# Loads on GpSimd's queue, and later operands in the model that orders TensorE: a scan and two layers on one core

## The chip, the core and the metric

The kernel runs on one core of a Trainium2 chip. The core has five engines that run side by side: TensorE (PE, matrix products; PEld is its loading of weights), VectorE (DVE), ScalarE (ACT), GpSimd (POOL) and SyncE (SP), which issues DMAs. Each engine takes its instructions in the order in which they stand in its queue, and waits for semaphores at the head of it. The metric is the device time in microseconds of one execution; less is better.

## The reference

A chunked scan over 4 x 8 sequences of 768 steps (head size 32, state size 16, chunks of 32), then two layers with a hidden width of 2048 over the 3072 tokens of width 256:

```
per chunk:  L   = causal * exp(cum_i - cum_j)
            y   = ((C B^T) * L) x  +  (C state) * exp(cum)
            state = exp(sum la) * state + sum_j B_j x_j exp(cum_end - cum_j)
x1 = leaky(y  @ w_in)  @ w_out          # leaky(h) = max(0.01 h, h)
x2 = relu(x1 @ w2_in)^2 @ w2_out
```

All inputs and the output are float32.

## The kernel before

The tokens are cut into 12 pieces of 256, three to a sequence group; in each piece 16 chunks of 32 steps lie side by side in 128 partitions. `scan_piece(p)` loads two tensors (in1: B, C, x; in2: decays and B), scales them by powers of two so that each is the sum of two half-precision parts, and has three groups of small products on TensorE: the **attention product** (L632 and L633, from the diagonal tile kbd into S), the **inside product** (L675 to L677, from xbh and xbl into Y) and the **carried product** (L714 and L715, from sbd into Y). The diagonal tiles hold blocks of 32 x 32 on a diagonal, so that one product serves four chunks; from piece 1 on, SyncE fills each with a group of four DMAs (`diag`, L556), and piece 0 does it with copies on DVE and ACT. The result of a piece goes to yh and yl (ACT L721 the rounded part, DVE L726 the rest), which the layers read. `sequence_scales` loads a whole sequence group five times in parts (L453) for its largest values.

The layers run in phases over one piece (256 tokens) or two (512). A phase has rounds of first products into hp (L761 to L763), the activation on ACT and DVE (gh, t, gl), second products into o (L792 and L793) and last products (L799). Every float32 product is made of three products of rounded parts; the weights are loaded as words (`load_w`, L294), and split by ACT (L309, L315, L353) and DVE (L328, L332, L357) into a rounded part and the rest.

The order of all this is not written by hand. `Plan.op` records each operation with its engine, an estimate of its duration, what it reads and writes; `Plan.order` runs a model of the engines: an operation is ready at the end of what it reads plus HOP (0.12), each engine takes the ready operation that must be done earliest (`lateness`, less a lead of 30 or 10 us for the scan), and buffers come free when their last reader is done. The program is then issued in the order of that model, so each engine's queue holds its instructions in that order. In the model SyncE issues a load in 0.06 us, and a group of four diagonal copies is one operation of 2.6 us that keeps SyncE for 0.3. All DMAs stand in SyncE's queue.

## Time and profile before

| | us |
|---|---|
| median of 3 runs | 672.5 (670.22 to 672.55) |
| the profiled execution | 672.55, of which its span 670.8 |
| PE busy | 603.6 (90% of the span) |
| DVE, ACT busy | 418.2 (62%), 362.7 (54%) |
| POOL busy | 5.2 (1%) |
| mean granted clock of TensorE | 0.977 |

The span is from the first to the last instruction. A row of the timeline has its start, its duration, the engine, the line of the kernel, the operation, what it writes from what it reads, the shapes, how many were merged into the row, and in brackets how long the engine sat idle before it and what ended that. "DMA kbd<-kmx" as what ended a wait is the landing of a diagonal copy. A wait is put down to what came last.

### The profile page before, as it was taken

To read this page: it belongs to the slowest core of one execution; us is meant where nothing else is said; L and a number is where in the kernel's file an instruction comes from. 1 tells how busy PE (TensorE), PEld (TensorE's weight loads), DVE (VectorE), ACT (ScalarE), POOL (GpSimd) and SP (SyncE) were. 2 spreads that over 40 slices of the span, in tenths; PEclk is the share of its full clock that TensorE was granted. 3 is DMA by queue.
4 is the path that set the end of the run, shared out by engine and by line. 5 is a ranking of instruction groups with operands and counts; after the bars stand their busy time and mean duration, and the time that the engine had idled before them with its cause. 6 is when DMAs were issued, how large, how long until landed. Compare 5 with 4: busy or idle time off the path is not lost.

```text
span 670.8 us, 11009 instructions
## 1 busy us (share of the span) xinstructions
PE 603.6 (90%) x4248; PEld 514.4 (77%) x4248; DVE 418.2 (62%) x735; ACT 362.7 (54%) x639; POOL 5.2 (1%) x14
## 2 busy tenths in 40 slices
PE   1378779899999998989999979999989999999997
PEld 0277669798887898877888767888767888888885
DVE  8968968689888546688423758522765422444553
ACT  5967845658765444555444545444644444444442
POOL 3000000000000000000000000000000000000000
PEclk9997979899999999999999989999989999999999
DMA  8565662542133334443000143100210000000000
GB/s 325 185 155 168 188 176 48 148 80 86 49 52 102 100 85 84 128 91 43 30 31 1 41 89 38 40 32 1 49 16 9 0 32 0 1 0 1 33 0 32
DMA packets 111252, 46.46 MB, mean 69 GB/s; under 512 B 94304, under 2 KB 100064, under 8 KB 111200
## 3 DMA queue, kind: packets, MB, share of 16 engines
q1 hardware_dynamic: 111200, 45.76, 27.0%
q8 instruction: 33, 0.54, 0.3%
q14 instruction: 19, 0.16, 0.1%
HBM read 36.83 MB, written 3.15 MB: 60 GB/s over the span
## 4 chain that ended last, share of the span: by engine, by line
PE 66%; DMA 11%; DVE 10%; ACT 6%; SPq 4%; issue 3%; DVEq 0%; ACTq 0%
PE hp L761 11%; PE o L799 10%; PE hp L762 10%; PE hp L763 10%; PE o L792 10%; PE o L793 10%; SPq L556 4%; DMA sbd<-t 3%; DMA in<-in 3%; DMA kbd<-kmx 2%; DVE gl L780 1%; DMA wst<-w2o 1%; DMA wst<-w1o 1%; ACT wst L315 1%; ACT wst L309 1%
## 5 line engine op out<-in xcount | busy, mean ns | idle before, releaser
L780 DVE TENSOR_TENSOR gl<-t,gh 128x512 fp32r<-128x512 f32 x192 | 131.6, 687 | 128.0 <-ACT gh L774 84.5
L761 PE MATMUL hp<-yl,wh1i 128*128 128x256 f32 (+1 forms) x288 | 96.3, 334 | 3.9 <-DVE yl L726 2.1
L763 PE MATMUL hp<-yh,wl1i 128*128 128x256 f32 (+1 forms) x288 | 95.3, 331 | 0.2 <-DVE wl1i L357 0.2
L762 PE MATMUL hp<-yh,wh1i 128*128 128x256 f32 (+1 forms) x288 | 95.3, 331 | 0.0
L792 PE MATMUL o<-gh,wl1o 128*128 128x256 f32 (+1 forms) x288 | 89.6, 331 | 4.8 <-DVE wl1o L357 4.2
L779 ACT CAST gh<-t 128x512 fp32r<-128x512 f32 x96 | 58.9, 619 | 63.0 <-DVE t L778 46.5
L774 ACT ACTIVATE gh<-hp 128x512 fp32r<-128x512 f32 x96 | 57.4, 598 | 61.2 <-PE hp L763 31.5
L793 PE MATMUL o<-gh,wh1o 128*128 128x256 f32 (+1 forms) x288 | 88.3, 327 | 0.0
L775 ACT ACTIVATE t<-hp 128x512 f32<-128x512 f32 x96 | 57.0, 598 | 57.2 <-PE hp L763 56.2
L777 ACT ACTIVATE t<-hp 128x512 f32<-128x512 f32 x96 | 57.3, 598 | 51.7 <-PE hp L763 49.1
L778 DVE TENSOR_TENSOR t<-t 128x512 f32<-128x512 f32 x96 | 65.5, 688 | 30.9 <-ACT t L777 30.6
L792 PE MATMUL o<-gh,w2o 128*128 128x512 f32 x192 | 76.8, 400 | 0.0
L761 PE MATMUL hp<-yl,wh2i 128*128 128x512 f32 x192 | 76.6, 399 | 0.0
L793 PE MATMUL o<-gh,w2o 128*128 128x512 f32 x192 | 76.0, 396 | 0.0
L763 PE MATMUL hp<-yh,wl2i 128*128 128x512 f32 x192 | 75.7, 394 | 0.0
L762 PE MATMUL hp<-yh,wh2i 128*128 128x512 f32 x192 | 75.5, 393 | 0.0
L799 PE MATMUL o<-gl,wh1o 128*128 128x256 f32 (+1 forms) x288 | 63.8, 332 | 2.4 <-DVE gl L780 2.3
L761 PEld LDWEIGHTS hp<-yl,wh1i 128*128 128x128 f32 x288 | 57.6, 200 | 9.1 <-DVE yl L726 2.2
L792 PEld LDWEIGHTS o<-gh,wl1o 128*128 128x128 f32 x288 | 56.5, 196 | 10.0 <-DVE wl1o L357 4.8
L763 PEld LDWEIGHTS hp<-yh,wl1i 128*128 128x128 f32 x288 | 57.8, 201 | 4.7 <-DVE wl1i L357 0.4
L762 PEld LDWEIGHTS hp<-yh,wh1i 128*128 128x128 f32 x288 | 57.7, 200 | 4.3
L799 PE MATMUL o<-gl,w2o 128*128 128x512 f32 x192 | 60.8, 398 | 0.0
(124 smaller groups left out, 935.2 us busy)
## 6 DMA issues: line engine op xcount, KB each, us to landing
in<-in SPq DMA_DIRECT2D x12, 640.0 KB, 4.3
in<-in SPq DMA_DIRECT2D x12, 512.0 KB, 3.4
all<-in SPq DMA_DIRECT2D x15, 384.0 KB, 3.8
wst<-w1i SPq DMA_DIRECT2D x8, 512.0 KB, 5.5
wst<-w1o SPq DMA_DIRECT2D x8, 512.0 KB, 5.8
wst<-w2i SPq DMA_DIRECT2D x8, 512.0 KB, 4.0
out_t<-ob SPq DMA_DIRECT2D x12, 256.0 KB, 2.2
wst<-w2o SPq DMA_DIRECT2D x5, 512.0 KB, 3.6
```

Source lines behind the costliest of these rows:

```text
L761: nc.tensor.matmul(hp, wh, xl[:, :, k], start=(k == 0), stop=False)
L762: nc.tensor.matmul(hp, wh, xh[:, :, k], start=False, stop=False)
L763: nc.tensor.matmul(hp, wl, xh[:, :, k], start=False, stop=(k == KI - 1))
L774: op("ACT", 0.6, lambda: nc.scalar.activation(gh(), h(), AF.Lrelu), r=[h], w=[gh], busy=0.52)
L775: op("ACT", 0.6, lambda: nc.scalar.activation(t(), h(), AF.Lrelu), r=[h], w=[t], busy=0.52)
L777: op("ACT", 0.6, lambda: nc.scalar.activation(t(), h(), AF.Relu), r=[h], w=[t], busy=0.52)
L778: op("DVE", 0.69, lambda: nc.vector.tensor_tensor(t(), t(), t(), ALU.mult), w=[t])
L779: op("ACT", 0.62, lambda: nc.scalar.copy(gh(), t()), r=[t], w=[gh], busy=0.55)
L780: op("DVE", 0.69, lambda: nc.vector.tensor_tensor(gl(), t(), gh().bitcast(F32), ALU.subtract), r=[t, gh], w=[gl])
L792: nc.tensor.matmul(o[d]()[:, : self.n], wl, gh()[:, c], start=(m == 0), stop=False)
L793: nc.tensor.matmul(o[d]()[:, : self.n], wh, gh()[:, c], start=False, stop=False)
L799: nc.tensor.matmul(o[d]()[:, : self.n], wh, gl()[:, c], start=False, stop=(m == KO - 1))
```

## The change

Two things are changed. The loads of weights, of the sequence groups and of all pieces but the first are issued from GpSimd's queue in place of SyncE's; the model gets GpSimd as an engine that takes 1.0 us for each. And in the model, an operation of TensorE sees what another engine made not 0.12 us after its end but 2.0 us in the scan pieces from 1 on, and 0.4 us in the layers. SyncE keeps the loads of piece 0, the diagonal copies and the stores of the output. What each instruction computes is as before; added lines move the numbers of all lines behind them by 6 to 8.

```diff
+HOP_SCAN, HOP_LAYERS = 2.0, 0.4
 HOP = 0.12
...
-        o.lead = self.lead
+        o.lead, o.hop = self.lead, self.hop_pe
...
+    def hop(self, y, b):
+        if y.kb:
+            return HOP + 0.5
+        if y.engine == b.engine:
+            return -y.us if y.engine == "PE" else 0.0
+        return b.hop if b.engine == "PE" else HOP
+
...
-        free = {e: 0.0 for e in ("PE", "DVE", "ACT", "SP")}
+        free = {e: 0.0 for e in ("PE", "DVE", "ACT", "SP", "POOL")}
...
-                        at = max(
-                            ends[y] + HOP if y.engine != b.engine or y.kb else 0.0 if y.engine == "PE" else ends[y]
-                            for y in b.before
-                        )
+                        at = max(ends[y] + self.hop(y, b) for y in b.before)
...
-        op("SP", 0.06, lambda: nc.sync.dma_start(st(), w_dram[nm][sl]), w=[st], kb=512 if j is None else 256)
+        op("POOL", 1.0, lambda: nc.gpsimd.dma_start(st(), w_dram[nm][sl]), w=[st], kb=512 if j is None else 256)
...
-                nc.sync.dma_start(t(), all_[:, :, U * at : U * (at + 16)])
+                nc.gpsimd.dma_start(t(), all_[:, :, U * at : U * (at + 16)])
...
-            op("SP", 0.06, load, w=[t], kb=384)
+            op("POOL", 1.0, load, w=[t], kb=384)
...
-        op("SP", 0.06, lambda: nc.sync.dma_start(v(), in1[p]), w=[(v, k) for k in ("x", "b", "ct")], kb=640)
-        op("SP", 0.06, lambda: nc.sync.dma_start(w(), in2[p]), w=[(w, k) for k in ("az", "bt")], kb=512)
+        e, us, q = ("SP", 0.06, nc.sync) if p == 0 else ("POOL", 1.0, nc.gpsimd)
+        op(e, us, lambda: q.dma_start(v(), in1[p]), w=[(v, k) for k in ("x", "b", "ct")], kb=640)
+        op(e, us, lambda: q.dma_start(w(), in2[p]), w=[(w, k) for k in ("az", "bt")], kb=512)
...
     weights()
+    plan.hop_pe = HOP_SCAN
...
-    plan.lead = 0.0
+    plan.lead, plan.hop_pe = 0.0, HOP_LAYERS
```

What this does to the queues, at three places. DVE at the start, from the maxima of piece 0 (mx) on; lt and e are its two scans, behind the clip of the decays (d1e, in_122 or in_124), wst is the first weight. Before:

```order
L405 TENSOR_REDUCE mx<-in_120 128x1 x3
L590 TENSOR_SCALAR d1e<-in_122 128x16
L591 TENSOR_SCALAR in_122<-in_122 128x16x31
L592 MEMSET in_122 128x16
L250 TENSOR_REDUCE pm<-ident 128x1
L598 SCALAR_TENSOR_TENSOR lt<-in_122,delta 128x512
L491 TENSOR_REDUCE m_154<-S 3x1
L603 SCALAR_TENSOR_TENSOR e_156<-in_122,d1e 128x512
L492 TENSOR_SCALAR dg<-ident,m_154 3x3
L328 SCALAR_TENSOR_TENSOR wst<-wst 128x512
```

Now:

```order
L411 TENSOR_REDUCE mx<-in_120 128x1 x3
L256 TENSOR_REDUCE pm<-ident 128x1
L497 TENSOR_REDUCE m_148<-S 3x1
L498 TENSOR_SCALAR dg<-ident,m_148 3x3
L334 SCALAR_TENSOR_TENSOR wst<-wst 128x512
L505 TENSOR_SCALAR eb<-S 128x3
L597 TENSOR_SCALAR d1e<-in_124 128x16
L598 TENSOR_SCALAR in_124<-in_124 128x16x31
L599 MEMSET in_124 128x16
L508 TENSOR_SCALAR eb<-eb 128x3
L605 SCALAR_TENSOR_TENSOR lt<-in_124,delta 128x512
```

The first weight's merge moved ahead of the clip and of both scans. The second place is the queue of the loads while pieces 0 and 1 are scanned; wst are weights, and the numbers are those of the buffers. On SyncE before:

```order
L294 DMA wst_352<-w1i 128x2x256
L556 DMA kbd_95<-kmx_440 32x16x32 x4
L556 DMA xbh_93<-xh_442 32x16x32 x4
L556 DMA xbl_94<-xl_469 32x16x32 x4
L294 DMA wst_543<-w1o 128x512
L294 DMA wst_589<-w1i 128x2x256
```

On GpSimd now:

```order
L459 DMA all_154<-in1 128x3x256
L524 DMA in1_255<-in1 128x1280
L525 DMA in2_314<-in2 128x1024
L300 DMA wst_320<-w1i 128x2x256
L300 DMA wst_415<-w1o 128x512
L300 DMA wst_444<-w1i 128x2x256
L300 DMA wst_471<-w1o 128x512
```

The copies are gone from between the loads; they stand alone in SyncE's queue, and eight weights stand ahead of these rows in GpSimd's. The third place is TensorE where the attention product of piece 9 begins (L632, now L639). Before:

```order
L761 MATMUL hp_4818<-yl_2613,wh2i_114 128x512
L762 MATMUL hp_4818<-yh_2597,wh2i_114 128x512
L763 MATMUL hp_4818<-yh_2597,wl2i_115 128x512
L632 LDWEIGHTS kbd_95
L632 MATMUL S_4831<-ch_4752,kbd_95 128x32
L633 LDWEIGHTS kbd_95
L633 MATMUL S_4831<-cl_4768,kbd_95 128x32
```

Now:

```order
L799 MATMUL o0_4809<-gh_4799,w2o_1974 128x512
L800 MATMUL o0_4809<-gh_4799,w2o_1974 128x512
L799 MATMUL o1_4812<-gh_4799,w2o_1974 128x512
L800 MATMUL o1_4812<-gh_4799,w2o_1974 128x512
L806 MATMUL o0_4809<-gl_4825,w2o_1974 128x512
L806 MATMUL o1_4812<-gl_4825,w2o_1974 128x512
L639 LDWEIGHTS kbd_95
L639 MATMUL S_4855<-ch_4727,kbd_95 128x32
L640 LDWEIGHTS kbd_95
L640 MATMUL S_4855<-cl_4773,kbd_95 128x32
```

Before, the attention product stands right behind a first product of layer 2, and the second and last products of the first three rounds of that phase come after it; now these three rounds' second and last products stand ahead of it, and one first product less.

## Rows read from the trace of the kernel before

**Rows 1.** Windows: stretch, its length, busy us of each engine, PEclk, DMA share, GB/s.

```profile
32.70:150.00 117.30, 96.70 (x943) 92.18 (x944) 94.24 (x182) 75.44 (x138) 0.00 (x0) 0.91 0.54 135
150.00:510.00 360.00, 343.63 (x2511) 289.72 (x2510) 225.07 (x380) 192.00 (x343) 0.00 (x0) 0.99 0.25 57
510.00:671.00 161.00, 156.65 (x679) 127.30 (x677) 69.59 (x101) 69.52 (x116) 0.00 (x0) 1.00 0.03 10
```

**Rows 2.** Waits of PE: engine, tile, line, what ended them: us, times, longest.

```profile
PE S L632 <- DMA kbd<-kmx: 17.4, 6, 5.4
...
PE Y L714 <- DMA sbd<-t: 5.6, 9, 1.6
...
PE o L792 <- DVE wl1o L357: 4.2, 3, 2.8
PE Y L676 <- DVE mkl L665: 3.4, 5, 1.0
```

**Rows 3.** Timeline of PE: the rows ahead of which it waited longest.

```profile
48.90 0.58 PE L792 MATMUL o<-gh,wl1o 128*128 128x256 f32 x1 [2.81 <-DVE wl1o L357]
...
87.03 0.19 PE L632 MATMUL S<-ch,kbd 128*128 128x32 f16 x1 [5.43 <-DMA kbd<-kmx]
...
122.21 0.18 PE L632 MATMUL S<-ch,kbd 128*128 128x32 f16 x1 [3.24 <-DMA kbd<-kmx]
...
265.68 0.18 PE L632 MATMUL S<-ch,kbd 128*128 128x32 f16 x1 [2.65 <-DMA kbd<-kmx]
...
283.89 0.18 PE L714 MATMUL Y<-qh,sbd 128*128 128x32 f16 x1 [1.64 <-DMA sbd<-t]
...
291.95 0.18 PE L632 MATMUL S<-ch,kbd 128*128 128x32 f16 x1 [1.48 <-DMA kbd<-kmx]
...
392.10 0.18 PE L632 MATMUL S<-ch,kbd 128*128 128x32 f16 x1 [2.39 <-DMA kbd<-kmx]
...
492.56 0.18 PE L632 MATMUL S<-ch,kbd 128*128 128x32 f16 x1 [2.24 <-DMA kbd<-kmx]
```

**Rows 4.** Windows of the stretches behind two of these waits.

```profile
283.90:290.40 6.50, 6.50 (x56) 5.20 (x56) 6.50 (x12) 4.29 (x8) 0.00 (x0) 1.00 0.45 47
392.10:397.50 5.40, 5.40 (x45) 4.46 (x46) 2.75 (x7) 0.00 (x0) 0.00 (x0) 0.68 0.63 143
```

**Rows 5.** Timeline of SP (its first weight load) and of POOL (its last instruction).

```profile
1.65 0.69 SPq L294 DMA_DIRECT2D wst<-w1i  x1
...
5.79 0.15 POOL L254 MEMSET dec<- 128x32 f32 x1
```

**Rows 6.** Timeline of SP: the copy groups of piece 1, first row, and the next load.

```profile
34.16 2.73 SPq L556 DMA_DIRECT2D kbd<-kmx  x4
...
42.42 0.56 SPq L294 DMA_DIRECT2D wst<-w1o  x1
```

**Rows 7.** DMA issues: line, count, KB each, median us from issue to landing.

```profile
in<-in SPq DMA_DIRECT2D x12, 640.0 KB, 4.3
...
wst<-w2o SPq DMA_DIRECT2D x5, 512.0 KB, 3.6
...
kbd<-kmx SPq DMA_DIRECT2D x44, 32.0 KB, 2.1
```

**Rows 8.** Timeline of DVE (three rows) and PE (its first layer product).

```profile
9.54 0.67 DVE L328 SCALAR_TENSOR_TENSOR wst<-wst 128x512 int32<-128x512 int32 x1
...
24.08 1.58 DVE L405 TENSOR_REDUCE mx<-in 128x1 f32<-128x512 f32 x3
...
89.48 0.95 DVE L456 TENSOR_REDUCE mx<-all 128x1 f32<-128x768 f32 x1 [4.07 <-DMA all<-in]
...
32.72 0.58 PE L761 MATMUL hp<-yl,wh1i 128*128 128x256 f32 x1 [2.06 <-DVE yl L726]
```

**Rows 9.** Timeline of PE: first rows of two rounds of the layers.

```profile
381.14 0.40 PE L761 MATMUL hp<-yl,wh2i 128*128 128x512 f32 x1
...
383.94 0.40 PE L761 MATMUL hp<-yl,wh2i 128*128 128x512 f32 x1
```

More of the change, by code (lines that the diff above doesn't have):

```diff
@@ L73, in __init__ @@
         self.ops, self.writer, self.readers, self.tags = [], {}, {}, {}
-        self.lead = 0.0
+        self.lead, self.hop_pe = 0.0, HOP
     def op(self, engine, us, fn, r=(), w=(), busy=None, kb=0):
         o = Op(len(self.ops), engine, us, fn, busy, kb)
-        o.lead = self.lead
+        o.lead, o.hop = self.lead, self.hop_pe
         for k in (*r, *w):
```

## Prediction, made before the changed kernel was run

> **What bounds the kernel now.** I read the stages first [rows 1]. Up to 32.7 us the first scan piece and the first weights are still on their way. From 32.7 to 150 TensorE is busy 96.7 of 117.3 us at a mean granted clock of 0.91, from 150 to 510 it is busy 343.6 of 360, and from 510, after the last scan piece, 156.7 of 161, the rest being the last output; nothing in the change reaches that stage. So what can be won is 20.6 us of idle time up to 150, 16.4 us from 150 to 510, and the clock. The view of waits says for whom TensorE stood idle [rows 2]: the attention product of a piece for the diagonal copy of its keys (17.4 us in 6 waits), the carried product for the copy of the states (5.6 in 9), the inside product for DVE (3.4 in 5), and the second product of layer 1 for a weight (4.2 in 3). Nearly all of it is time in which layer products lay ready behind a scan product: TensorE takes its instructions in order, so where the scan product stands in that order decides whether the copy is hidden. The single waits are in [rows 3]. A second price hangs on them: after the wait of 2.39 us the stretch that follows ran at 0.68 of the full clock, so at the lower of its two levels, 1.2 GHz, for about 3.5 of its 5.4 us; after the wait of 1.64 us it stayed at 1.00 [rows 4].
>
> **1. The start.** All weights now stand in GpSimd's queue behind its set-up, which ends at 5.79 + 0.15 = 5.94 us; before, SyncE issued the first at 1.65 [rows 5]. What GpSimd needs to issue one load is in no row. The nearest from below is SyncE's 0.56 for one load, from above its 2.73 for a group of four diagonal copies [rows 6]; I take 1.0, nearer the lower end, since a load has 128 to 384 contiguous pieces and a group of copies 4 x 32 x 16 = 2,048. A load of this size lands 3.6 us after its issue where the wire is free [rows 7], so the first weight is there at 5.94 + 1.0 + 3.6 = 10.5 us (estimate; ends 10.1 and 12.3), ACT halves it in two operations of some 0.6, and DVE can merge it at 11.7 instead of 9.54 [rows 8]. What makes this dear is the new order on DVE: the merge now stands ahead of the clip and the two scans of piece 0, which before ran while the weight was coming. That is 2.2 us of waiting plus some 3.0 us of work that loses its cover, less the three weight operations and one product that stood ahead of the keys before (2.5 us). I take **+2.8** at the first layer product (32.72 before [rows 8]), ends 0 and +6.3.
>
> **2. Attention products moved back.** One round of the layers is six first products, four second and two last, 383.94 - 381.14 = 2.8 us [rows 9], half of it the first, a third the second, a sixth the last (the half-width products of layer 1, twice as many, are counted the same). I counted in both orders how much of this stands between a scan product and what it waits for, and set it against the wait of before [rows 3]. Pieces are numbered from 0. Piece 2 (wait 5.43): one round more, takes back 2.8. Piece 3 (3.24): the same amount after the carried product of piece 2 as before; this wait is made by three copy groups issued one after another on SyncE, 2.6 each, and a landing of 2.1 [rows 6, 7], so at least 3 x 2.6 + 2.1 = 9.9 us after the states' copy of the piece before began to free SyncE, against some 7 us of products; I take back 1.7, because the loads no longer stand between the groups. Piece 6 (2.65): 1.9 us more behind its scales, takes back 1.9. Piece 7 (1.48): 1.9 more, all 1.5. Piece 9 (2.39): 2.8 more counted from piece 8's attention product but 2.2 less counted from its carried product, which frees the keys' buffer; the scales of this sequence now come before that carried product, where before ACT and DVE waited for them; I take back 1.7. Piece 11 (2.24): 2.3 more, all 2.2. Together 2.8 + 1.7 + 1.9 + 1.5 + 1.7 + 2.2 = 11.8: **-11.8**, ends -3.0 and -17.4.
>
> **3. Carried and inside products.** They stand 1.4 to 3.2 us of layer products later behind the product before them in nearly every piece. The 1.64 us of piece 6's carried product [rows 3] and most of the rest of the 5.6 + 3.4 [rows 2] are each shorter than that; I take back 7.2 of 9.0: **-7.2**, ends -3 and -9.
>
> **4. Loads out from behind the diagonal copies.** SyncE issued the copies of piece 1 from 34.16 to 42.3 and only then, at 42.42, the load of a weight whose buffer had been free [rows 6]. ACT, in order, stood before that weight, and TensorE waited 2.81 us at 48.90 for an earlier one behind it on ACT [rows 3]. In GpSimd's queue no copy stands ahead. I take back the 2.8 and 0.4 of the other two (4.2 in 3 [rows 2]): **-3.2**, ends 0 and -4.2. DVE, too, stood 4.07 us before a load for the scales of the next sequence [rows 8] that was queued behind the key copies; what that gives is in the second rival. The Trainium skill, "DMA: Bandwidth & Descriptors", section Issuing engines are not separate DMA queues, speaks against this step: DMAs of all engines share the same DMA engines, and issuing from several saves only the sequencer's issue time. By that rule this term is about nothing and the sum 3.2 higher, 658.6. The rows speak for more [rows 6]: what the load lost was not its own 0.56 us but a place 8.2 us further back. No run here shows it yet.
>
> **5. The clock.** Three late waits of over 2.2 us (pieces 6, 9, 11) each cost about 0.32 x 5.4 = 1.7 us at the lower level [rows 4]; with under 1 us of wait left there I take all three: **-5.1**, ends 0 and -8.5 (with two more of the same size after pieces 2 and 3).
>
> **6. New waits.** Up to 110 us the pieces follow one another through ACT and DVE, which are busy 75.4 and 94.2 of 117.3 us [rows 1] and whose work per piece is not less. There a scan product that stands later only moves the wait. Piece 1's carried product has two first, one second and two last products more ahead of it, but its attention product also comes some 5.6 us later (2.8 of the start, 2.8 of one round), and its chain with it: I put +5 there, between nothing and those 5.6. After the carried products of pieces 2 and 3 only 1.9 us of products stand before the first that reads the piece's result, in which ACT and DVE must round the result and take the rest, one step each of some 0.7 behind the product's own 0.9: +1.4 and +1.0. And +0.5 for piece 7, which the next phase reads 3.2 us later. **+7.9**, ends 0 and +11.
>
> Sum: 2.8 - 11.8 - 7.2 - 3.2 - 5.1 + 7.9 = -16.6 us. The profiled execution took 672.55 us (span 670.8 and 1.75 around it), beside a median of 672.5: 672.55 - 16.6 = **655.9 us**.
>
> **Rivals.** *The scan chain slides along.* The next piece's keys need the buffer that the carried product of the piece before frees, so placing carried products later delays the next attention product by as much. For: the count from carried to attention product shrinks for pieces 5 and 9. Against: pieces 7 and 11 gain 1.9 and 2.3 by the same count. Then the waits of pieces 3, 6 and 9 stay as they are (1.7 + 1.9 + 1.7 = 5.3 not won), and so do the three clock drops (5.1): 655.9 + 10.4 = 666.3 us.
>
> *The first 150 us loosen too.* With the loads ahead, DVE's 4.07 us [rows 8] vanish, the pieces come earlier, and the new waits do not arise: 655.9 - 7.9 - 2 = 646 us. Against: DVE is 94.2 / 117.3 = 80% busy there, and the start is later.
>
> *Slower: GpSimd issues too slowly.* Nine loads (eight weights, one for scales) stand in its queue ahead of piece 1's operands. At g us each these are issued at 5.94 + 9g. In the trace they were read by DVE at 24.08 and land in some 4.3 us [rows 7, 8], so from g = (19.8 - 5.94) / 9 = 1.5 each further 0.1 us costs 0.9 us of the start, and every later piece's loads are slowed as well. The forecast's gain is gone at 1.5 + 16.6 / 9 = 3.4; at 4.0 the time is 655.9 + 9 x 2.5 = 678 us. For: no row shows g, and a load has up to three rows in each partition. Against: SyncE's dearest group of four with far more pieces took 2.73 [rows 6]. The Trainium skill, "SBUF — State Buffer", section SBUF: two separate sides, names a way to a large g: GpSimd cannot write descriptors while DVE runs an operation in a two-port mode. No row shows it here.
>
> *The table does nothing.* That the order is not what the table says is excluded: the orders differ as shown. No change within 0.5% (3.4 us, about what a measurement can tell from none) would need the first rival together with the dear ends of the start and of the new waits: 666.3 + 3.5 + 3.1 = 673 us.
>
> **Chances.** Forecast (650 to 661) 0.50; everything loosens, 646, 0.18; the chain slides, 666, 0.20, of which a quarter ends within 0.5%; no change 0.05; slow issue 0.07. Faster by over 0.5%: 0.50 + 0.18 + 0.15 = 0.83; within: 0.05 + 0.05 = 0.10; slower 0.07. The range takes in the second rival and most of the first: 644 to 668, which leaves out some 0.05 below and 0.13 above.
>
> **What would show it.** In the trace after: the first weight operation on ACT near 10.5 us (from 8.23) and the first layer product near 35.5; GpSimd's DMA issues some 1 us apart (over 1.5 would speak for the slow issue); waits of TensorE for the key copies down from 17.4 to some 6 us, and for the state copies to about 2; a clock of 1.00 in the stretches after pieces 6, 9 and 11; in 150 to 510 us TensorE idle for less than 4 us per 360. The steps on the early pieces are wrong if TensorE's idle time up to 150 us differs from 20.6 by more than 8 either way. The forecast is wrong if key copies are still waited for over 12 us in all, or if a new wait for a load appears on TensorE, ACT or DVE that is longer than those it replaces.

## The result: slower by 1.4%, and the profile after

The changed kernel took 681.71 us (median of 4 runs, 681.37 to 682.93) beside 672.52 us (670.22 to 673.71) of the kernel before in the same sitting: ratio 1.0144, 95% interval 1.0114 to 1.0174. The forecast was 655.9, the range 644 to 668; the change makes the kernel slower by 9.2 us. One of the four runs of e12 below (689.0 us) fell in a slower state of the chip and is left out of its median; all other medians are of fast runs.

Windows of the changed kernel by stage, columns as in [rows 1]:

```profile
32.70:150.00 117.30, 91.68 (x855) 86.97 (x852) 93.91 (x187) 75.93 (x139) 19.21 (x30) 0.83 0.57 144
150.00:510.00 360.00, 343.66 (x2477) 293.32 (x2476) 220.46 (x375) 189.00 (x340) 18.42 (x30) 0.97 0.27 56
```

Up to 150 us TensorE is busy 5.0 us less than in [rows 1], and at a granted clock of 0.83 instead of 0.91; from 150 to 510 us it is idle as long as before (16.3 us), at 0.97 instead of 0.99. Nothing of the forecast 16.6 us shows up.

Waits of TensorE in the changed kernel (engine, tile, line, what ended them: us in total, times, longest), to be read against [rows 2]; lines have moved by 7 there (L632 is L639, L714 is L721):

```profile
PE S L639 <- DMA kbd<-kmx: 17.9, 6, 4.5
PE Y L721 <- DMA sbd<-t: 5.8, 2, 3.0
PE Y L684 <- DMA xbl<-xl: 5.6, 1, 5.6
```

The key copies (kbd) are waited for as long as before although the products that read them stand later in TensorE's order, the state copies (sbd) too, and a third kind is new: the copies of x (xbl). Together TensorE waits 29.3 us for copies; before it was 17.4 + 5.6 = 23.0 [rows 2]. The single waits, from the timeline of TensorE:

```profile
61.91 0.20 PE L684 MATMUL Y<-mkh,xbl 128*128 128x48 f16 x1 [5.60 <-DMA xbl<-xl]
...
288.88 0.18 PE L639 MATMUL S<-ch,kbd 128*128 128x32 f16 x1 [4.53 <-DMA kbd<-kmx]
```

What happened to the copies is best seen in DMA issues of the changed kernel (count, KB each, median us from issue to landing), beside 2.1 us for kbd in [rows 7]; xbl landed in 2.1 before as well:

```profile
kbd<-kmx SPq DMA_DIRECT2D x44, 32.0 KB, 2.8
...
xbl<-xl SPq DMA_DIRECT2D x44, 32.0 KB, 2.3
```

And at the longest wait, in the timelines of SyncE and GpSimd around the copies of piece 1's xbl:

```profile
49.10 4.73 SPq L563 DMA_DIRECT2D xbl<-xl  x4
...
46.95 0.72 POOL L300 DMA_DIRECT2D wst<-w1i  x1 [6.28 <-DVE rr L446]
48.76 0.55 POOL L524 DMA_DIRECT2D in<-in  x1 [1.09 <-DVE e L643]
50.21 0.53 POOL L300 DMA_DIRECT2D wst<-w1o  x1 [0.90 <-DVE wl1o L363]
53.42 0.53 POOL L525 DMA_DIRECT2D in<-in  x1 [2.68 <-DVE mkl L672]
54.05 0.73 POOL L300 DMA_DIRECT2D wst<-w1i  x1
```

Five loads of 512 to 640 KB were issued from GpSimd's queue within 7.1 us around a copy group that SyncE issued in 4.73 us, where a group takes 2.6 to 2.7 [rows 6]; it had landed only at 61.91, 8.1 us after its issue ended (49.10 + 4.73). From this came the theories that the experiments were to tell apart: **A**, the copies are late because the loads, in another queue, now move at the same time; **B**, the new order costs the time and the queue is harmless (with **E**, it is the late start); **C**, the waits only slide with the order; **F**, GpSimd's loads themselves come too late.

### The profile page after: what moved, and what is told of

Read it like the earlier page. It is cut to its first block, busy times and chain, and to the rows that moved or that the text cites. A ratio compares the mean times of both kernels' runs of the same rounds, so it can differ in the third digit from the quotient of the medians.

```text
span 681.2 us, 11019 instructions
## 1 busy us (share of the span) xinstructions
PE 607.8 (89%) x4248; PEld 520.2 (76%) x4248; DVE 417.6 (61%) x735; ACT 362.5 (53%) x639; POOL 50.6 (7%) x86
## 3 DMA queue, kind: packets, MB, share of 16 engines
q0 software_dynamic: 9504, 35.66, 17.0%
q1 hardware_dynamic: 94944, 10.10, 10.5%
## 4 chain that ended last, share of the span: by engine, by line
PE 54%; DMA 3%; SPq 2%; DVE 1%; ACT 0%; issue 0%
PE hp L768 9%; PE o L799 9%; PE o L806 9%; PE o L800 9%; PE hp L770 8%; PE hp L769 8%; DMA all<-in 2%; DMA kbd<-kmx 2%; SPq L563 2%; PE S L639 0%; PE Y L682 0%; PE S L640 0%; PE Y L683 0%; PE Y L684 0%; PE Y L721 0%
## 5 line engine op out<-in xcount | busy, mean ns | idle before, releaser
L768 PE MATMUL hp<-yl,wh1i 128*128 128x256 f32 (+1 forms) x288 | 97.8, 340 | 3.6 <-DVE yl L733 3.1
L799 PE MATMUL o<-gh,wl1o 128*128 128x256 f32 (+1 forms) x288 | 91.8, 337 | 2.5 <-DVE yl L825 1.3
L800 PE MATMUL o<-gh,wh1o 128*128 128x256 f32 (+1 forms) x288 | 90.4, 333 | 0.0
L770 PE MATMUL hp<-yh,wl2i 128*128 128x512 f32 x192 | 76.2, 397 | 0.0
L799 PE MATMUL o<-gh,w2o 128*128 128x512 f32 x192 | 75.7, 394 | 0.0
L800 PE MATMUL o<-gh,w2o 128*128 128x512 f32 x192 | 74.8, 390 | 0.0
L806 PE MATMUL o<-gl,wh1o 128*128 128x256 f32 (+1 forms) x288 | 64.9, 336 | 5.5 <-DVE gl L787 5.5
L768 PEld LDWEIGHTS hp<-yl,wh1i 128*128 128x128 f32 x288 | 59.0, 205 | 8.9 <-DVE yl L733 3.1
L799 PEld LDWEIGHTS o<-gh,wl1o 128*128 128x128 f32 x288 | 58.5, 203 | 7.5 <-DVE yl L825 1.6
L769 PEld LDWEIGHTS hp<-yh,wh1i 128*128 128x128 f32 x288 | 59.2, 206 | 4.3
L800 PEld LDWEIGHTS o<-gh,wh1o 128*128 128x128 f32 x288 | 58.5, 203 | 4.4
```

The lines of the kernel that those rows point to most:

```text
L768: nc.tensor.matmul(hp, wh, xl[:, :, k], start=(k == 0), stop=False)
L769: nc.tensor.matmul(hp, wh, xh[:, :, k], start=False, stop=False)
L770: nc.tensor.matmul(hp, wl, xh[:, :, k], start=False, stop=(k == KI - 1))
L799: nc.tensor.matmul(o[d]()[:, : self.n], wl, gh()[:, c], start=(m == 0), stop=False)
L800: nc.tensor.matmul(o[d]()[:, : self.n], wh, gh()[:, c], start=False, stop=False)
L806: nc.tensor.matmul(o[d]()[:, : self.n], wh, gl()[:, c], start=False, stop=(m == KO - 1))
```

## Experiments

All medians are of the same kind as above; ratios are against runs of the kernel before on the same chip. "Copies" is the sum of TensorE's waits for diagonal copies, "all waits" that of all rows of its view of waits but those put down to "issue", "busy" its busy time, in the profiled execution; the same products at a lower clock make busy longer.

| kernel | order of work | loads on GpSimd's queue | us | ratio, 95% interval | copies | all waits | busy |
|---|---|---|---|---|---|---|---|
| before | old | none | 672 | 1 | 23.0 | 62.3 | 603.6 |
| changed | new | all | 681.7 | 1.0114 to 1.0174 | 29.3 | 68.3 | 607.8 |
| e1 | old | all | 689.3 | 1.0231 to 1.0304 | 33.2 | 76.0 | 603.5 |
| e2 | new | none | 666.8 | 0.9885 to 0.9942 | 10.8 | 58.8 | 602.9 |
| e4 | later operands alone | none | 661.2 | 0.9821 to 0.9865 | 11.6 | 56.8 | 598.6 |
| e5 | new without later operands | all | 683.7 | 1.0156 to 1.0208 | 33.7 | 74.4 | 600.2 |
| e6 | new | weights | 666.5 | 0.9919 to 0.9958 | 15.5 | 61.2 | 598.7 |
| e7 | new | operands, scales | 672.5 | 0.9999 to 1.0036 | 22.1 | 66.2 | 598.7 |
| e11 | new | all, wait for copies | 690.4 | 1.0242 to 1.0305 | 16.4 | 76.2 | 608.8 |
| e12 | new | all, ring twice | 677.0 | 1.0052 to 1.0211 | 28.4 | 69.9 | 601.2 |
| e13 | new | all, short operands | 667.7 | 0.9910 to 0.9963 | 25.1 | 64.9 | 600.1 |
| e14 | new | none, short operands | 662.9 | 0.9846 to 0.9897 | 11.0 | 57.5 | 599.0 |
| e8 | scan operands alone, 2.0 | none | 662.3 | 0.9847 to 0.9887 | 9.0 | 55.7 | 599.6 |
| e15 | the same, 2.6 | none | 661.7 | 0.9832 to 0.9875 | 7.2 | 56.6 | 598.6 |
| e10 | scan 4.0, layers 0.4 | none | 670.8 | 0.9962 to 1.0008 | 1.7 | 63.8 | 599.3 |

### The change in its halves

e1 moves the queue and keeps the old order:

```diff
-        op("SP", 0.06, lambda: nc.sync.dma_start(st(), w_dram[nm][sl]), ...
+        op("SP", 0.06, lambda: nc.gpsimd.dma_start(st(), w_dram[nm][sl]), ...
...
-                nc.sync.dma_start(t(), all_[:, :, U * at : U * (at + 16)])
+                nc.gpsimd.dma_start(t(), all_[:, :, U * at : U * (at + 16)])
...
+        q = nc.sync if p == 0 else nc.gpsimd
+        op("SP", 0.06, lambda: q.dma_start(v(), in1[p]), ...
...
```

> The kernel before with its order of work kept (its table of numbers unchanged), only that the weights, the loads for the scales and the operands of pieces 1 to 11 are issued from GpSimd's queue. Theory A (the diagonal copies, left alone on SyncE's queue, now move at the same time as the big loads and land later): slower than before by 5 to 20 us; TensorE's waits for the key copies grow from 17.4 us to over 22, and the copies whose issue meets loads take 3 to 5 us to issue and over 4 us to land, where the others keep 2.6 and 2.1. Theory B (the new order is what costs; the queue is harmless): within 4 us of before, the difference being the start (up to +2.8), and waits for the key copies of 15 to 19 us. Theory C (loads free of the queue loosen the kernel, and the new order wastes that): faster by 3 us or more.

e2 is the reverse, the changed kernel with each `nc.gpsimd.dma_start` put back to `nc.sync.dma_start` while the model still believes the loads on POOL:

```diff
-        op("POOL", 1.0, lambda: nc.gpsimd.dma_start(st(), w_dram[nm][sl]), ...
+        op("POOL", 1.0, lambda: nc.sync.dma_start(st(), w_dram[nm][sl]), ...
...
```

> The changed kernel with the order of work of the change kept exactly, only that every load is issued from SyncE's queue as before. Theory A: the order does what the prediction said, less the start and less the loads that no longer stand behind copies; faster than before by 6 to 20 us (653 to 667), key copies waited for 5 to 10 us in all. Theory B: slower than before by 3 to 12 us, with the waits of the early pieces as in the changed kernel (a wait of over 3 us for an operand of piece 1 and one of over 2.5 us for the keys of pieces 2 and 3). Theory C (waits only slide with the order): within 4 us of before, key copies waited for 14 to 19 us.

e4 takes from the change the later operands; the loads are on SyncE, in the model as well. It also keeps two lines of the changed model that the account of the change above does not name, though its diff shows them: what a load brings is seen 0.5 us later than before (`HOP + 0.5`), by every engine, and an operation of TensorE that needs an earlier one of TensorE is ready when that one starts (`-y.us`), where before it had not to wait for it at all. So do e5, e8, e15 and e10, and no run takes these lines apart; "later operands" below means all of it.

```diff
+HOP_SCAN, HOP_LAYERS = 2.0, 0.4
...
+    plan.hop_pe = HOP_SCAN
...
-    plan.lead = 0.0
+    plan.lead, plan.hop_pe = 0.0, HOP_LAYERS
```

> The kernel before with one half of the change: in the model TensorE's operands come later (2.0 us for scan products, 0.4 for the layers), while the model still has the loads on SyncE at 0.06 us and they are issued there. Theory A: faster than before by 6 to 20 us, as in the run with the order alone and without its costs at the start (first layer product near 33 us). Theory B: slower than before by 2 us or more. Theory C: within 4 us of before.

e5 is the rest of the change without them:

```diff
-HOP_SCAN, HOP_LAYERS = 2.0, 0.4
 HOP = 0.12
+HOP_SCAN, HOP_LAYERS = HOP, HOP
```

> The other half of the change: loads issued from GpSimd's queue and modelled there at 1.0 us each, but TensorE's operands come at 0.12 us after their producer for all products, as before. Theory A: the slowest of the four, 8 to 25 us slower than before (the copies land late and the products do not stand later to cover that), key copies waited for over 22 us. Theory B: within 4 us of before if the later operands are the costly part of the order. Theory C: faster than before by 2 us or more.

Measured: 689.3, 666.8, 661.2 and 683.7. The queue costs 17.0 us in the old order (e1 against the 672.3 beside it) and 14.9 in the new one (changed against e2); the later operands without the rest of the change gain 11.1 us (e4); the model's belief that loads stand on POOL at 1.0 us costs 5.6 in the order that it makes (e2 against e4; which operation there costs it was not taken apart). Together -11.1 + 5.6 + 14.9 = +9.4; the change measured +9.2, which is no check, since the three are steps of one chain from the kernel before to the changed one. The shares hold for this chain alone: with the loads on GpSimd's queue the numbers 2.0 and 0.4 gain only 2.0 us (e5 against the changed kernel), and the model's belief, which is then true, gains 5.6 together with the two lines named above (e1 against e5). B and C fall with e2 and e4. Theory A's numbers hold but for three: e2 gained 5.5, its lower end being 6, its key copies were waited for 10.8 us, the upper end being 10, and e5 is not the slowest, e1 is. Waits of TensorE for key copies, in e1 and in e2:

```profile
PE S L633 <- DMA kbd<-kmx: 28.4, 6, 6.5
```

```profile
PE S L639 <- DMA kbd<-kmx: 10.8, 5, 3.6
```

In e2 TensorE runs through the same list of products as in the changed kernel. At piece 1 the timelines of SyncE (the copies, the first and the last of the five loads) and of TensorE read:

```profile
46.08 3.08 SPq L563 DMA_DIRECT2D xbl<-xl  x4
49.26 0.60 SPq L300 DMA_DIRECT2D wst<-w1i  x1
...
51.54 0.60 SPq L300 DMA_DIRECT2D wst<-w1i  x1
```

```profile
51.81 0.18 PE L684 MATMUL Y<-mkh,xbl 128*128 128x48 f16 x1
```

The same five loads stand behind the copies in SyncE's list, the first is issued when the last copy has been, and the product that waited 5.60 us in the changed kernel does not wait at all. The four copies of xbl land there in 2.7 us (median), in the changed kernel in 8.7.

This longest wait is not where most of the time went, though. Since the two lists are the same, the kernels can be compared product by product. The layer product that the changed kernel starts at 158.84 starts in e2 at 156.38; the attention product that it starts at 320.18 starts in e2 at 305.38. Of the 15.3 us between the two profiled executions (spans of 681.2 and 665.9), 2.5 lie ahead of the first of these products, 12.3 between them and 0.5 behind. Windows from the one to the other, in the changed kernel and in e2:

```profile
158.84:320.18 161.34, 148.84 (x1192) 134.30 (x1193) 107.21 (x188) 83.33 (x158) 14.70 (x23) 0.95 0.34 77
```

```profile
156.38:305.38 149.00, 145.34 (x1192) 130.40 (x1193) 106.76 (x188) 83.22 (x158) 0.00 (x0) 0.99 0.33 79
```

The same products take 3.5 us more at the lower clock, and TensorE idles 12.5 us instead of 3.7. The longest wait in there is the 4.53 us for the keys of piece 6. Timelines of SyncE and GpSimd of the changed kernel ahead of it:

```profile
281.38 3.57 SPq L563 DMA_DIRECT2D kbd<-kmx  x4
...
280.53 0.57 POOL L524 DMA_DIRECT2D in<-in  x1 [2.76 <-DVE gl L787]
282.21 0.75 POOL L459 DMA_DIRECT2D all<-in  x1 [1.11 <-DVE mx L462]
```

The keys land at 288.88, 3.9 us after their issue ended. In e2 SyncE issues the same two loads at 275.38 and 276.05, behind the copies of these keys (269.08) and of xbl (272.68), and TensorE waits 1.80 us for the keys.

### Which loads

e6 puts the operands of the pieces and the loads for the scales back on SyncE and leaves the weights on GpSimd; e7 is the opposite. Both keep the new order.

```diff
-                nc.gpsimd.dma_start(t(), all_[:, :, U * at : U * (at + 16)])
+                nc.sync.dma_start(t(), all_[:, :, U * at : U * (at + 16)])
...
-        e, us, q = ("SP", 0.06, nc.sync) if p == 0 else ("POOL", 1.0, nc.gpsimd)
+        e, us, q = ("SP", 0.06, nc.sync) if p == 0 else ("POOL", 1.0, nc.sync)
```

> The changed kernel with its order, with only the weights issued from GpSimd's queue; the operands of pieces 1 to 11 and the loads for the scales go from SyncE's. The order with all loads on SyncE took 666.8 us, with all on GpSimd 681.7. Theory A (any load that moves beside the copies delays them): between the two, 671 to 679, since the weights move only up to about 110 us. Rival E (the start is what costs, that is the first weight at 10.5 us): 678 to 682, nearly the whole.

> The changed kernel with its order, with only the operands of pieces 1 to 11 and the loads for the scales issued from GpSimd's queue; all weights go from SyncE's. Theory A: between 666.8 and 681.7, 671 to 679, and with the weights alone on GpSimd the two excesses add up to about 15 us; late copies in 150 to 510 us as in the changed kernel (a wait of some 4 us for the keys of piece 6). Rival E: 665 to 669, since the weights are back on the queue that issues the first of them at 1.65 us.

Measured: 666.5 and 672.5. The weights alone cost nothing that can be told beside e2's 666.8 (the intervals overlap), which theory A had not expected, although the first layer product comes as late as in the changed kernel (34.17 beside 34.78, in e2 32.20); so the start (E) is not it either. The operands alone cost 5.7, within theory A's range, and the wait for the keys of piece 6 is there as forecast (4.34 us), but the two excesses do not add up to 15. Between the two products named above e6 loses 2.7 us to e2 and e7 7.7, of the changed kernel's 12.3. Ahead of the first of them e6 and e7 are 4.5 and 3.7 us before e2 and the changed kernel 2.5 behind; why the two sorts of loads together cost more there than each by itself is not shown. The landing of the key copies changes with the operands and not with the weights: in e6 its median is 2.1 us as before, in e7 (DMA issues) it is

```profile
kbd<-kmx SPq DMA_DIRECT2D x44, 32.0 KB, 3.0
```

The median is no measure of the loss: it is 2.8 in the changed kernel, which is 9.2 us slower than e7.

### Copies beside loads, by themselves

e3 appends trials to the kernel before; a group of copies reads `src`, and each trial ends when copies and loads have landed:

```diff
+        for _ in range(2):
+            trial()
+            trial(long_rows, nc.sync)
+            trial(None, nc.sync, long_rows)
+            trial(long_rows, nc.gpsimd)
+            trial(long_rows, nc.scalar)
+            trial(short_rows, nc.gpsimd)
+            trial(long_rows, nc.gpsimd, copy=False)
```

> The kernel before, whole, and behind its last product fourteen trials one after another, each waiting for the end of the one before; the time of the whole is of no interest. A trial is one group of four diagonal copies on SyncE's queue (2,048 pieces of 64 bytes) and two weight loads of 512 KB (rows of 2 KB). In turn: 1 the group alone; 2 both loads ahead of it in SyncE's queue; 3 both loads behind it in SyncE's queue; 4 both loads on GpSimd's queue at the same moment; 5 both on ScalarE's queue at the same moment; 6 both on GpSimd's queue with the rows cut into pieces of 256 bytes; 7 the two loads on GpSimd's queue without copies. Then all again. Read is the time from the start of the group's issue to the end of its issue, and to its landing. Theory A (whatever queue they come from, transfers of two queues share the DMA engines, and the copies get the smaller part beside long rows): trial 1 2.6 and 4.7 us; trials 2 and 4 and 5 alike, landing at 7 us or later; trial 3 within 1 us of trial 1, since nothing is ahead of the copies; trial 6 lands earlier than 4 by over 1 us. Theory A' (only GpSimd's queue does it): trial 4 as above, trial 5 like trial 1. Rival D (the copies are not slowed by the transfers at all, what is late in the changed kernel is only their start): trials 4 and 5 within 0.7 us of trial 1.

ScalarE reads what the first copy of the group wrote, so the start of its cast is that copy's landing. Trials 1, 3 and 4, and the second time of trial 5, in the timeline of e3 (issue of the copies by SyncE, cast by ScalarE):

```profile
667.07 2.64 SPq L884 DMA_DIRECT2D kbd<-psrc  x4
669.25 0.62 ACT L900 CAST pgot<-kbd 128x512 f32<-128x512 f16 x1 [3.11 <-DMA kbd<-psrc]
...
677.15 2.62 SPq L884 DMA_DIRECT2D kbd<-psrc  x4
679.28 0.62 ACT L900 CAST pgot<-kbd 128x512 f32<-128x512 f16 x1 [2.62 <-DMA kbd<-psrc]
...
685.77 2.76 SPq L884 DMA_DIRECT2D kbd<-psrc  x4
691.55 0.62 ACT L900 CAST pgot<-kbd 128x512 f32<-128x512 f16 x1 [11.66 <-DMA kbd<-psrc]
...
750.79 2.84 SPq L884 DMA_DIRECT2D kbd<-psrc  x4
755.66 0.62 ACT L900 CAST pgot<-kbd 128x512 f32<-128x512 f16 x1 [5.36 <-DMA kbd<-psrc]
```

| | first copy lands after | second time |
|---|---|---|
| 1 copies alone | 2.2 | 2.1 |
| 2 two loads ahead in SyncE's queue | 4.2 | 4.5 |
| 3 two loads behind in SyncE's queue | 2.1 | 2.1 |
| 4 two loads from GpSimd | 5.8 | 5.6 |
| 5 two loads from ScalarE | 4.8 | 4.9 |
| 6 loads from GpSimd in pieces of 256 bytes | 2.2 | 2.2 |

The copies land 2.7 to 3.6 us later beside loads of another queue, whichever engine issued these (theory A, not A' and not D), and 2.0 to 2.4 us later behind them in the same queue. Trial 3 shows less than it seems to: the first copy had landed (679.28) before SyncE issued the first load (679.82). The group of four as a whole landed after 4.2 to 4.3 us in trial 1, after 5.7 in trial 5, and after at most 5.2 in trial 2 and 6.5 in trial 4, so the 7 us expected for it were too much; its issue was not slowed (2.6 to 2.9). Trial 6 is no proof that short rows are harmless: GpSimd issued those loads one by one, 2.2 to 3.3 us idle between them, so that only some 128 KB moved beside the copies.

What holds the copies up shows in their packets. DMA queues in the first time of trial 5, in the 3.0 us from the start of the copies' issue (q10 is ScalarE's queue) and in the 1.8 us from 695.7 on (q1 is SyncE's; packets, MB, share of the 16 DMA engines):

```profile
q10 hardware_dynamic: 253, 0.97, 95.5%
```

```profile
q1 hardware_dynamic: 2112, 0.13, 82.5%
```

In those first 3.0 us no packet of SyncE's queue moved at all, where the first copy alone had landed after 2.2. So here the copies were not slowed as they moved: they began to move when nearly all of the two loads (1.05 MB) had. (The loads' packets are of 4 KB here, 237 of the 253 for the 0.97 MB, not rows of 2 KB as expected.) In trial 4, beside GpSimd's loads, they did mix: 1,210 of the copies' 2,112 packets moved before the loads had ended.

The Trainium skill, "DMA: Bandwidth & Descriptors", section Queues, rings and completion order, says that each DMA engine takes turns between the queue rows that have work for it, a packet from one and then one from the next. Trial 5 agrees with that only if such a packet holds a large part of a load, since 253 of what the profile counts as packets went ahead of the copies' first. How large a packet is in the skill's sense, no run here shows.

### Loads that wait for the copies, and a larger ring

e11 keeps all loads on GpSimd's queue and lets GpSimd read an element of each copy group, so that what is behind waits; e12 doubles the memory for GpSimd's descriptors.

```diff
+    hold = cp.tile([P, 1], F16, name="hold")[96:128]
...
                 for h in range(4):
                     nc.sync.dma_start(dst[quad[h], :, h, :], shape(src())[quad[h]])
+                nc.gpsimd.tensor_copy(hold, dst[quad[3], 0, 3, 0:1])
```

> The changed kernel with its order and with all loads still on GpSimd's queue, and one addition: after each group of diagonal copies GpSimd copies one element of the last of them, so that the loads behind it in its queue start only when these copies have landed. Theory A (the copies are late because loads move beside them): faster than the changed kernel's 681.7 by 5 to 14 us (668 to 677), though GpSimd now waits, and TensorE's waits for copies fall from 29.3 us in all to under 21. Rival F (loads on GpSimd's queue come late, because its queue of descriptors takes few at a time; the copies are only held up with all else): slower than the changed kernel by 2 us or more, since every load now comes later still.

```diff
-    nc = bacc.Bacc("TRN2", target_bir_lowering=False, num_devices=1, dynamic_dma_scratch_size=1024)
+    nc = bacc.Bacc("TRN2", target_bir_lowering=False, num_devices=1, dynamic_dma_scratch_size=2048)
```

> The changed kernel with the memory for GpSimd's descriptors doubled (2048 instead of 1024 bytes in each partition), so that about twice as many of its loads can be under way at once. Rival F: faster than the changed kernel's 681.7 by 4 us or more, above all at the start, where GpSimd stood 1.4 to 2.8 us between two loads. Theory A: the start gains 1 to 2 us at most, and with more loads beside the copies the whole is between 1 us faster and 5 us slower.

e11 took 690.4, where theory A expected 668 to 677: a miss, and what rival F had forecast. The copies did what A says: they land in 2.0 us again (median of kbd; it was 2.8), and TensorE waits 16.4 us for copies instead of 29.3. But TensorE's other waits rose by more, from 39.0 to 59.8. Waits in e11, of GpSimd, DVE and ScalarE:

```profile
POOL hold L565 <- DMA sbd<-t: 122.0, 11, 17.4
POOL hold L565 <- DMA kbd<-kmx: 36.7, 11, 6.8
```

```profile
DVE mx L463 <- DMA all<-in: 19.2, 9, 5.0
```

```profile
ACT ch L594 <- DMA in<-in: 21.6, 4, 10.5
```

GpSimd stands before a copy that is not even issued yet, and loads whose buffers are free wait behind it; DVE's waits for the scales' loads rose from 7.3 to 19.2 us. In SyncE's list a load waits only until the copies ahead of it have been issued. e12's runs took 676.6, 677.0, 684.7 and 689.0 beside the changed kernel's 681.7. The gaps between GpSimd's first loads went, and two runs gain over 4 us, where F began, but the interval of its ratio holds that of the changed kernel: no gain is shown, and none excluded. In the profiled execution (677.0) what is gained lies ahead of the two products named above: they start at 152.08 and 314.57, 162.5 us apart, where it was 161.3 in the changed kernel and 149.0 in e2. TensorE still waits 28.4 us for copies. So the ring is not what makes these late, nor what costs the time where most of it was lost. What e11 adds is that loads which come late cost more here than was won on the copies.

### Fewer bytes beside the copies

```diff
+    vp = sp.tile([P, U * (N + T + D)], F32, tag="in1", name="vp", bufs=1)
+    wq_ = sp.tile([P, U * 2 * T], F32, tag="in2", name="wq_", bufs=1)
...
+        v.make, w.make = lambda: vp, lambda: wq_
...
-        op(e, us, lambda: q.dma_start(v(), in1[p]), ...
-        op(e, us, lambda: q.dma_start(w(), in2[p]), ...
+        op(e, us, lambda: q.dma_start(v(), in1[p]) if p == 0 else q.dma_start(v()[:, 0:320], in1[p][:, 0:320]), ...
+        op(e, us, lambda: q.dma_start(w(), in2[p]) if p == 0 else q.dma_start(w()[:, U * T :], in2[p][:, U * T :]), ...
```

> The changed kernel with its order, all loads on GpSimd's queue, but of the operands of pieces 1 to 11 only 416 of 1,152 KB are moved, with as many instructions and as many pieces (a quarter of each row of the first operand, half of the second); the rest of these tiles keeps the values of the piece before, so the result isn't the reference's. To be read against the next run, the same with all loads on SyncE's queue; with full operands the two stood 14.9 us apart (681.7 and 666.8). Theory A (the bytes that move beside the copies make them late): this run at 668 to 676, under 9 us above the next one. If not the bytes but the issuing or the order of arrival on GpSimd's queue is what costs: 676 to 682, still 11 us or more above the next one.

> The same short operands with the order of the change and all loads on SyncE's queue. Both theories: 662 to 667, a little under the 666.8 with full operands, because there the copies had loads only ahead of them in the same queue.

Measured: 667.7 (662.5 to 671.3) and 662.9. The first is a little under theory A's range, the second within its own. With 64% of the operands' bytes gone the queue costs 4.8 us instead of 14.9, and GpSimd issues as many loads as before, in 0.53 to 0.57 us each for the operands. So two thirds of the loss come from what moves beside the copies, not from the issuing on GpSimd. Bytes and packets are not told apart by this: with the bytes the packets of GpSimd's queue fell too, from 9,504 to 7,744. The median landing of kbd is 2.1 us in e14; in the DMA issues of e13 it is

```profile
kbd<-kmx SPq DMA_DIRECT2D x44, 32.0 KB, 2.3
```

One thing does not fit: TensorE's waits for copies in e13 are still 25.1 us. What fell most beside the changed kernel is its busy time (607.8 to 600.1), so much of the gain came back through the clock. Its profiled execution is also the slowest of its ten (671.25). Full weights still move beside the copies there; why they alone do no harm in e6 and some in e13 stays open.

### How much later the operands should come

Three kernels with all loads on SyncE and other numbers in one line:

```diff
-HOP_SCAN, HOP_LAYERS = 2.0, 0.4
+HOP_SCAN, HOP_LAYERS = 2.0, 0.12
```

> The kernel with all loads on SyncE's queue and the model's 2.0 us for operands of scan products, but the layers' products at 0.12 us as before (with 0.4 it took 661.2 us; with neither 672.3). If the gain is that scan products stand further behind their copies, as the prediction's steps 2 and 3 say, it is kept: 658 to 664. If it is the layers' 0.4 us that loosen the chains of the layers, it is lost: 669 to 674.

> All loads on SyncE's queue, 2.6 us for the operands of scan products in the model, layers as before at 0.12. Between the runs with 2.0 (662.3, waits for copies 9.0 us) and with 4.0 (670.8, copies 1.7 us, but new waits for what the scan makes). If the optimum is flat: 658 to 664. If products standing later than their copies need already cost: 664 to 669.

> All loads on SyncE's queue, the model's later operands for scan products doubled to 4.0 us (layers 0.4): with 2.0 it took 661.2 us, and TensorE still waited 11.6 us in 6 for key copies. If placing scan products still later goes on hiding these waits, 653 to 659; if the waits then move to what reads the scan's result (the chain of a piece slides along), 662 to 668.

Measured: 662.3, 661.7, 670.8. The 0.4 us of the layers do nothing (662.3 and 661.2), 2.6 is as good as 2.0, and 4.0 gives nearly everything back, more than either of its two forecasts: copies are waited for 1.7 us in all, and what the scan makes, and the weights, take their place. Waits of TensorE in e10 (the same view of before has 2.1 for yl, and for the weight 4.2 [rows 2]):

```profile
PE hp L768 <- DVE yl L733: 13.9, 4, 5.6
PE o L799 <- DVE wl1o L363: 12.6, 4, 7.6
PE Y L721 <- ACT sbd L572: 6.8, 1, 6.8
```

e4, 661.2 us (0.9821 to 0.9865), beats both kernels, and e8 and e15 do as well: it is the change without its queue.

## Why the prediction was wrong, step by step

- **Step 4, loads out from behind the copies: the step that failed.** It stood at -3.2, with ends 0 and -4.2; measured, moving the loads costs +14.9 (new order) to +17.0 (old order). The step counted what the loads gain by leaving SyncE's queue and never what the copies lose by losing that queue's order. [rows 6] were read the wrong way round: the load that stood 8.2 us behind the copies was, by standing there, kept off the wire while they moved, and TensorE waited for copies more than for loads. The waits for the weight wl1o did fall from 4.2 to 1.2, but the copies' landing rose from 2.1 to 2.8 us and their waits from 23.0 to 29.3. The prediction's own sign that it is wrong, key copies waited for over 12 us, came true (17.9). The other sum of that step, by the rule of the Trainium skill, "DMA: Bandwidth & Descriptors", section Issuing engines are not separate DMA queues, that issuing from several engines saves only issue time, should read 659.1 (655.9 + 3.2) and not 658.6; it missed the sign too, though it stands nearer.
- **Steps 2 and 3, products moved back: right for half the pieces, seven tenths in size.** With the loads on SyncE (e4) the copies' waits fall from 23.0 to 11.6, and those of the inside product for DVE from 3.4 to 1.0: 13.8 us, where the two steps had 19.0. What is missing lies in pieces 3, 6 and 9, where 5.3 were to be won and nothing was: 3.24, 2.65 and 2.39 us before [rows 3], and in the timeline of TensorE in e4

```profile
124.29 0.18 PE L639 MATMUL S<-ch,kbd 128*128 128x32 f16 x1 [4.02 <-DMA kbd<-kmx]
...
267.81 0.19 PE L639 MATMUL S<-ch,kbd 128*128 128x32 f16 x1 [2.32 <-DMA kbd<-kmx]
...
390.65 0.18 PE L639 MATMUL S<-ch,kbd 128*128 128x32 f16 x1 [2.08 <-DMA kbd<-kmx]
```

  These are the waits that the first rival, the sliding chain, said would stay. With loads on GpSimd the new order leaves 29.3: the products were moved back by what a copy took in the trace of before, and the change made the copy longer.
- **Step 5, the clock: -5.1, and -5.0 in e4** by TensorE's busy time (603.6 to 598.6), but the match is luck. The stretches behind pieces 6 and 9, two of the three that the step counted, still ran at 0.68 of the full clock in e4, as [rows 4] have it for piece 9; most of the 5.0 came from elsewhere:

```profile
267.81:273.21 5.40, 5.40 (x57) 5.40 (x58) 2.00 (x4) 0.00 (x0) 0.00 (x0) 0.68 0.72 173
390.65:396.05 5.40, 5.40 (x45) 4.45 (x46) 5.40 (x12) 3.06 (x5) 0.00 (x0) 0.68 0.36 117
```

  In the changed kernel it went the other way, +4.2. After the new waits of 5.60 us (xbl), 3.04 (piece 5's states) and 4.53 (piece 6's keys) the windows of the changed kernel show the lower level, 1.2 GHz, for the whole or most of 5 to 6 us:

```profile
61.90:67.90 6.00, 5.99 (x65) 6.00 (x66) 3.44 (x6) 3.93 (x7) 0.72 (x1) 0.50 0.01 3
243.00:248.00 5.00, 4.98 (x51) 5.00 (x52) 2.50 (x5) 1.77 (x3) 0.76 (x1) 0.50 0.55 180
288.90:295.00 6.10, 6.10 (x60) 5.96 (x61) 5.07 (x8) 2.65 (x4) 0.57 (x1) 0.65 0.04 6
```

- **Step 6, new waits: +7.9, and +8.3 in e4.** All waits but those for copies went from 62.3 - 23.0 = 39.3 to 56.8 - 11.6 = 45.2, and the 2.4 won for DVE, counted above, is in that. The size is right, the parts only in part. The waits for the scan's yl behind pieces 2 and 3 are 0.34 and 2.11 us in e4, together what the step put there (1.4 and 1.0, though its working, 0.9 + 0.7 + 0.7 less 1.9, gives 0.4 each). The +5 on piece 1 is not there, its carried product waits for nothing; in its place TensorE waits longer for gl (6.4 us, before 2.3) and for the layers' yl (4.8, before 0.7). So in e4 the steps read -13.8 - 5.0 + 8.3 = -10.5 (time -11.1) against -16.2 in the sum: of the 5.7 between them 5.2 are copies that still come late.
- **Step 1, the start: right, though it did not reach the end.** First weight operation on ScalarE at 10.50 (forecast 10.5), DVE's merge at 11.74 (11.7), first layer product at 34.78, so +2.1 for a forecast of +2.8 (its own terms, 2.2 + 3.0 - 2.5, make 2.7). e6 starts its layers as late and is as fast as e2, which starts them at 32.20.
- **The rivals.** Slow issue on GpSimd did not happen (0.53 to 0.91 us a load, forecast 1.0), so the one slower case that was priced was the wrong one: the slower case was not in what the loads need, but in what they do to the queue that they left. The sliding chain named the waits that e4 did not win (pieces 3, 6 and 9); that they stay because the keys' buffer comes free later was not tested, and its price, 666.3, is not what the changed kernel took. The loose start did not come. What 4.0 us shows (e10) is step 6 grown large.
- **The order made for loads on POOL: a term that the sum lacked**, +5.6 with the loads on SyncE (e2 against e4), -5.6 with them on GpSimd (e5 against e1, where the two other lines of the model change as well). Of its parts only the start was priced.

What remains: of the 15.3 us between the profiled executions of the changed kernel and e2, which run the same order (14.9 by the medians), 9.5 are waits (68.3 - 58.8; those for copies are 18.5 more, the others 9.0 less) and 4.9 are busy time at a lower clock (607.8 - 602.9). That the queue costs this time is shown (e1 against before, the changed kernel against e2), and so is that copies land later beside loads (e3, and the landings in e1, e7 and the changed kernel). That the late copies are the whole of the loss is not, since e6 shows weights beside copies without loss and e13 keeps most of the waits. What part of it is GpSimd's own is open too: beside its loads the copies of e3 land 0.7 to 1.0 us later than beside ScalarE's, and no run put the kernel's loads on ScalarE's queue.

## What to carry to other kernels

A queue is also an order: in these runs big loads that stood behind small urgent copies in one queue were kept off the wire for them, and moving the loads to another engine's queue set the two side by side. Before such a move, list what stays in the old queue, who waits for it, and how many bytes will now move beside it. If a model sets the order, change its numbers and its queues in separate runs; here the new numbers gained 11 us and the queue with its place in the model lost 20 on top of that; one run of both at once shows only the 9 between them.

## What the runs showed of the hardware that was not expected

- A copy of 64-byte pieces that lands in 2.1 to 2.2 us took 4.8 to 4.9 beside two loads of 512 KB from ScalarE's queue and 5.6 to 5.8 beside the same from GpSimd's (e3). Beside ScalarE's none of the copies' packets moved in the first 3.0 us.
- GpSimd stood idle between loads that nothing in the program held back. In the changed kernel's timeline of GpSimd:

```profile
10.80 0.73 POOL L300 DMA_DIRECT2D wst<-w1i  x1 [2.29 <-issue]
...
17.52 0.91 POOL L459 DMA_DIRECT2D all<-in  x1 [2.83 <-issue]
```

  With twice the memory for descriptors (e12) the ninth load is issued at 11.02 instead of 17.52:

```profile
11.02 0.78 POOL L459 DMA_DIRECT2D all<-in  x1
```

  Yet the first attention product came only 0.4 us earlier (19.1 and 19.5), and no gain of the whole is shown. In e3 loads cut into 512 pieces went one at a time, with 2.2 to 3.3 us idle between them.
